# Chunked attention before a routed MoE: window rows of two heads interleaved over the partitions, memory values and sums by one product, and another way from the last gate to the first gather

## The chip, the cores and the metric

The kernel runs on one core of a Trainium2 chip. The metric is device time in microseconds (us) of one execution; smaller is better. TensorE (PE), VectorE (DVE), ScalarE (ACT), GpSimd (POOL) and SyncE (SP) each work through their own instructions in order, and 16 DMA engines serve the queues into which SP, ACT and POOL put transfers. TensorE's granted clock is shown by the profile as a share of full speed.

## The reference

Two stages follow each other. The first is attention over chunks: q, k and v are 4 batches of 8 heads, 768 tokens of 64 values. Each chunk of 32 queries looks at 8 memory rows and a window of 56 tokens around it (16 to the left, its own 32, 8 to the right; cut at the ends), 64 keys in all.

```python
for c in range(nc):                     # 24 chunks of 32
    k_full = np.concatenate([mem_k, k[:, :, l_start:r_end]], axis=2)
    v_full = np.concatenate([mem_v, v[:, :, l_start:r_end]], axis=2)
    scores = scale * np.matmul(q_c, k_full.transpose(0, 1, 3, 2))
    a = np.exp(scores - np.max(scores, axis=-1, keepdims=True))
    a = a / (np.sum(a, axis=-1, keepdims=True) + 1e-09)
    out[:, :, c_start:c_end] = np.matmul(a, v_full)
```

Its output, 3072 tokens of 512 values, goes into a router: `noisy = x @ w_gate + log1p(exp(x @ w_noise)) * noise`; the best two of 8 experts are taken, their weights are a softmax over the two, and each token's result is the weighted sum of `relu(x @ w1[e]) @ w2[e]` (512 to 1024 to 512) over its two experts.

## The kernel before, in words

**Attention** runs in 12 iterations, i = 0 to 11: three per batch, each of 256 tokens (two tiles of 128), all 8 heads. Heads go in pairs; the parity of a head within its pair is `par`.

Loads of v, q and k of a batch are POOL's DMAs (L117, `load_v`, `load_kq`). For v, POOL copies the rows into another order (`spread_v`, L357, two copies), SP writes that to a scratch in DRAM (`vd`, L363), and POOL's DMAs read it back as windows (`window_v`, L372: four per batch, 32 or 24 rows x 24 chunks x 256 values). In the window tile `vb` a head of parity 0 owns partitions 0 to 63 and one of parity 1 owns 64 to 127: 8 memory rows, then 56 window rows; the other half of the columns is zero. The memory rows come by two more POOL DMAs per batch (L367), which copy them from a small tile `mvn` once for every chunk. POOL's own order is written out: every instruction is kept in program order.

TensorE, ScalarE, VectorE and SP follow the order of the program in the loop (`manual_schedule`). For iteration i, TensorE does the scores of i + 1 (`scores`: 8 products with the memory keys, L397, and 32 on 32 columns of the array each, L404), the transposes of the probabilities of i (L425), the transposes of x of i - 1 (L459), the products of `values` for i (8 sums against a two-column tile of ones, L436; 32 products of 32 columns, L442), and the gate of i - 1 (L469, 8 narrow products). In between, `fill` puts the transposes that bring the next batch's q and k into place (L382). VectorE takes the maximum (L412), subtracts it (L414), takes the reciprocal of the sums (L446), multiplies the products by it (L449, twice), copies the gate's logits (L471) and has the routing's small steps. ScalarE does the exponential (L419) and the copies of transposes out of PSUM (L428, L461). Rows of x go to a scratch in DRAM, `xd` (L476), from which the second stage gathers.

The sums have their own tile of PSUM (`small`), which holds the gate's logits as well, at other columns; the products have `ps_o`.

**The way to the gathers.** Tokens are routed in four groups (`Route`: r0, ra, rb with tiles 14 to 19, rc with tiles 20 to 23). Each chooses its two experts (`choose`: 14 small steps of VectorE ending in the one-hot of the pair of experts, `ohp`, L278), takes ranks within a pair by products with triangular and full ones (L284 to L288), turns a rank into a one-hot over 128 places (`slots`, L328, VectorE), spreads six facts per token over the pairs (`values`, L334) and sums them into lists by products (L341). `total` (L318, L322) adds the group's counts to a running count `cum`. The lists are decoded into row numbers to gather (`main_src`, L483) and to write (`main_dst`, L488). r0 and ra are done during the attention, most of rb and all of rc after it. The first gather (L654) waits for `main_src`.

**The MoE** gathers 28 tiles, one per pair of experts, transposes them and does two products for each expert (L697, L709), with results added and written by POOL's indirect DMAs (L660).

The tiles that the change touches are `vb`, `mvn`, `small`, `ps_o`, `rs`, `xd`, `facts`, `vals`, `oh_l` and `listed`.

Of the kernel before, what the change touches and what calls it, by code (L numbers as in the profile page):

```python
# [22 lines left out]
def kernel(  # L23
# [74 lines left out]
    xd = tc.dram_tile([N, Dm // 2], I32, name="xd")  # L98
# [13 lines left out]
    mvs = w_all[0:B * NM, 0, 0:2 * H * D].bitcast(F32).rearrange("p (h d) -> p h d", h=H)  # L112
# [23 lines left out]
    psG = actx.enter_context(tc.psum_pool(name="psG", bufs=1))  # L136
# [15 lines left out]
    for i in range(2):  # L152
        for r0, n in ((0, LC), (LC + S, CH - LC)):
            nc.sync.dma_start(out=vd[i][r0:r0 + n, :], in_=zeros[0:n, :])

# [5 lines left out]
    for b in range(B):  # L161
        nc.sync.dma_start(out=mvs[b * NM:(b + 1) * NM], in_=mem_v[b].rearrange("h m d -> m h d"))
    mvn = keep.tile([B * NM, Dm], BF16, name="mvn")
# [8 lines left out]

    ones2 = const.tile([128, 2], BF16, name="ones2")
    nc.vector.memset(ones2, 0.0)
    nc.vector.memset(ones2[0:64, 0:1], 1.0)
    nc.vector.memset(ones2[64:128, 1:2], 1.0)

# [21 lines left out]
    nc.gpsimd.iota(facts[:, :, 1], pattern=[[1, NG]], base=1, channel_multiplier=0, allow_small_or_imprecise_dtypes=True)  # L199
# [17 lines left out]
    for par in range(2):  # L217
        nc.scalar.copy(vb[1][own(par), 1 - par].rearrange("p (x c) w -> p x (c w)", x=NCH // 2),
                       zeros[own(par), :].unsqueeze(1).to_broadcast([64, NCH // 2, Dm]))
# [9 lines left out]
    class Route:  # L229
# [11 lines left out]
        def noise(self):  # L241
            self.ns = self.tile("ns", E).rearrange("p (n e) -> p n e", e=E)
            nc.scalar.activation(out=self.ns, in_=self.lg[:, :, E:2 * E], func=Act.Exp)
            nc.scalar.activation(out=self.ns, in_=self.ns, func=Act.Ln, bias=1.0)
# [46 lines left out]

        def weights(self, eng):
# [36 lines left out]

        def values(self, eng, lo, hi):  # L330
# [30 lines left out]
    def window_v(b):  # L361
        t, o = vb[b % 2], vd[b % 2]
        nc.sync.dma_start(out=o[LC:LC + S, :].rearrange("(p s) c -> p (s c)", s=SO), in_=vp)  # L363
        for par in range(2):
            p0 = par * 64
            cols = slice(par * 256, (par + 1) * 256)
            pin(nc.gpsimd.dma_start(out=t[p0:p0 + NM, par], in_=mvn[b * NM:(b + 1) * NM, cols].unsqueeze(1).to_broadcast([NM, NCH, 256])))  # L367
        for par in range(2):
            p0 = par * 64
            cols = slice(par * 256, (par + 1) * 256)  # L370
            for r0, n in ((0, CH), (CH, WIN - CH)):
                pin(nc.gpsimd.dma_start(out=t[p0 + NM + r0:p0 + NM + r0 + n, par],  # L372
                                        in_=o[r0:r0 + S, cols].rearrange("(c k) w -> k c w", k=CH)[0:n]))
# [15 lines left out]
    small = psG.tile([128, 4, 128], F32, name="small")  # L389
# [27 lines left out]
    def exps(sc):  # L417
        pb = work.tile([128, 2 * HP, 2, KW], BF16, name="pb")
        nc.scalar.activation(out=pb.rearrange("p x a w -> p (x a) w"), in_=sc, func=Act.Exp, scale=scale)  # L419
        return pb  # L420

    def turn_p(pb):
        p_p = bank([128, 2 * HP, 128], BF16, name="p_p")
        for x in range(2 * HP):
            nc.tensor.transpose(out=p_p[:, x, :], in_=pb[:, x].rearrange("p a w -> p (a w)"),  # L425
                                identity=identb)
# [4 lines left out]
    def values(t, pT, between=None):  # L431
        b, tp = divmod(t, TP)
        ps_g = small[:, t % 2, 0:2 * H].rearrange("p (j h) -> p j h", j=2)
        for x in range(2 * HP):
            j, pair = divmod(x, HP)
            nc.tensor.matmul(out=ps_g[:, j, 2 * pair:2 * pair + 2], lhsT=pT[:, x, :], rhs=ones2,  # L436
                             start=True, stop=True)
        ps_o = psO.tile([128, 2, HP, 2, D], F32, name="ps_o")
        for j in range(2):
            for pair in range(HP):  # L440
                for r in range(4):
                    nc.tensor.matmul(out=ps_o[r * CH:(r + 1) * CH, j, pair], lhsT=pT[:, j * HP + pair, r * CH:(r + 1) * CH],  # L442
                                     rhs=vb[b % 2][:, :, (tp * 2 + j) * 4 + r, pair * D:(pair + 1) * D],
                                     start=True, stop=True, tile_position=(0, r * CH))
        rs = work.tile([128, 2, H], F32, name="rs")
        nc.vector.reciprocal(rs, ps_g)  # L446
        xr = xrow[b % 2][:, 2 * tp:2 * tp + 2]
        for j in range(2):
            nc.vector.tensor_tensor(out=xr[:, j, 0:Dm].rearrange("p (h d) -> p h d", h=H),  # L449
                                    in0=ps_o[:, j].rearrange("p c a d -> p (c a) d"), in1=bc(rs[:, j], D), op=Alu.mult)  # L450
# [4 lines left out]
    def turn_x(xr):  # L455
# [5 lines left out]
        nc.scalar.copy(xT, p_x)  # L461
        return xT

    def gate(t, xT):
        b, tp = divmod(t, TP)
        ps_l = small[:, 2 + t % 2, 0:4 * E].rearrange("p (j e) -> p j e", j=2)
        for j in range(2):
            for kp in range(KP):
                nc.tensor.matmul(out=ps_l[:, j, :], lhsT=xT[:, kp, j, :], rhs=wgn[:, kp, :],  # L469
                                 start=(kp == 0), stop=(kp == KP - 1))  # L470
        nc.vector.tensor_copy(lg_all[:, 2 * t:2 * t + 2, :], ps_l)  # L471

    def keep_x(t, q):
        b, tp = divmod(t, TP)
        g0 = b * SO + 2 * tp
        q.dma_start(out=xd[g0 * 128:(g0 + 2) * 128, :].rearrange("(s p) r -> p s r", p=128),  # L476
                    in_=xrow[b % 2][:, 2 * tp:2 * tp + 2].bitcast(I32))

    def decode(L, n, name):
        t = const.tile([128, n], F32, name=f"{name}_t")  # L480
        nc.vector.scalar_tensor_tensor(out=t, in0=L[:, 1], scalar=128.0, in1=L[:, 0], op0=Alu.mult, op1=Alu.add)
# [486 lines left out]
```

## Time and profile before

| | us |
|---|---|
| median of three executions | 369.55 (367.07 to 370.01) |
| the profiled execution | 367.86 |
| its span | 366.2 |
| first window product (L442) | 32.46 |
| last normalisation (L449) starts | 134.62 |
| first gather is issued (L654) | 147.20 |
| first product of the MoE (L697) | 151.38 |

The profile is one execution. Its page has busy times by engine, 40 slices of the span with a digit per slice for each engine, for the granted clock and for the DMA engines, and groups of instructions by line, with how long one takes and what ended the idle time before it. The trace answers narrower questions: stretches of time, what each engine waited for, a timeline. In the timeline a row gives the start, the time, the engine, the line, what is written from what, the shape, how many instructions the row holds, and in brackets the idle time before it with its releaser. `PEld` is TensorE's loading of weights, which runs beside its products. Line numbers are those of the kernel before.

### The profile page before, as it was taken

What the parts mean: (1) busy time and instruction counts of PE and PEld (TensorE: products, weight loads), DVE (VectorE), ACT (ScalarE), POOL (GpSimd) and SP (SyncE); (2) the same over time, 40 slices, a digit from 0 to 9 for tenths busy, and PEclk for the clock granted to TensorE, in tenths of its full rate; (3) what the DMA queues carried; (4) which work ended last, traced back from release to release, by engine and by line L of the source; (5) the groups of instructions that cost most, each with busy time, mean ns of one, the idle gap of its engine ahead of it and who ended that gap; (6) DMA issues with size and microseconds to landing.
All of it is one profiled execution on the core that took longest, in us unless ns stands there. A gap on an engine that the chain in (4) does not pass through costs nothing.

```text
span 366.2 us, 7045 instructions
## 1 busy us (share of the span) xinstructions
PE 282.3 (77%) x2941; PEld 181.3 (50%) x2941; DVE 171.0 (47%) x344; ACT 136.7 (37%) x189; POOL 134.9 (37%) x181
## 2 busy tenths in 40 slices
PE   0347373766817752599999999999989999999992
PEld 0236363555715641565554455764436675565540
DVE  7656274699766989431223300964300233312231
ACT  8714554463644360034333243222234223234310
POOL 6460473336435014742651453352480032201122
PEclk9995656685775885599999999999999999999997
DMA  8999999999999999379999999991299982100012
GB/s 115 247 155 169 248 162 155 258 199 199 237 176 198 228 225 180 80 147 179 159 186 206 250 184 240 101 215 54 69 154 186 193 185 80 52 2 2 24 43 81
DMA packets 55462, 56.97 MB, mean 156 GB/s; under 512 B 20119, under 2 KB 45783, under 8 KB 55424
## 3 DMA queue, kind: packets, MB, share of 16 engines
q0 software_dynamic: 34240, 46.82, 73.9%
q1 hardware_dynamic: 14048, 6.62, 9.5%
q10 hardware_dynamic: 7136, 3.02, 4.3%
q8 instruction: 25, 0.41, 0.5%
q14 instruction: 13, 0.11, 0.1%
HBM read 70.39 MB, written 13.96 MB: 230 GB/s over the span
## 4 chain that ended last, share of the span: by engine, by line
issue 25%; PE 21%; POOL 8%; DVE 5%; DMA 2%; POOLq 1%; ACT 0%; another core or an unknown queue 0%; DVEq 0%
PE p_h L697 10%; PE p_y L709 9%; POOL out_dram L660 6%; DMA out_dram<-y,main_dst 1%; POOL xt L654 1%; DMA xt<-xd,main_src 1%; PE p_xt L674 1%; DVE h L683 1%; POOL w_all L826 0%; DVE cum L322 0%; DVE w_all L449 0%; POOLq L963 0%; ACT xT L461 0%; DVE oh_l L328 0%
## 5 line engine op out<-in xcount | busy, mean ns | idle before, releaser
L709 PE MATMUL p_y<-w_all,h 128*128 128x512 bf16 x464 | 103.9, 379 | 1.5 <-ACT y L713 1.5
L697 PE MATMUL p_h<-xTt,w_all 128*128 128x256 bf16 (+3 forms) x672 | 102.9, 313 | 1.1 <-issue 0.5
L697 PEld LDWEIGHTS <-w_all 128*128 128x128 bf16 x736 | 69.8, 100 | 37.1 <-issue 1.6
L685 ACT ACTIVATE h<-p_h 128x512 bf16<-128x512 f32 (+1 forms) x81 | 44.5, 551 | 98.6 <-PE p_h L697 90.7
L709 PEld LDWEIGHTS <-h 128*128 128x128 bf16 x464 | 45.3, 98 | 53.2 <-issue 1.8
L683 DVE TENSOR_SCALAR h<-p_h 128x512 bf16<-128x512 f32 (+1 forms) x49 | 31.0, 632 | 85.9 <-PE p_h L697 70.5
L660 POOL DMA_INDIRECT out_dram<-y,main_dst x28 | 30.8, 1101 | 86.0 <-DVE y L715 75.6
L382 PE MATMUL p_t<-identb,w_all 128*64 128x128 bf16 x384 | 19.3, 272 | 30.8 <-DMA w_all<-in_k_dram 14.8
L715 DVE SCALAR_TENSOR_TENSOR y<-p_y,main_w,y 128x512 f32<-128x512 f32 x28 | 21.0, 750 | 37.9 <-PE p_y L709 33.3
L654 POOL DMA_INDIRECT xt<-xd,main_src x28 | 27.5, 982 | 26.3 <-DMA xTt<-xt 13.3
L713 ACT ACTIVATE y<-p_y,main_w 128x512 f32<-128x512 f32 x28 | 19.1, 687 | 38.8 <-PE p_y L709 35.6
L382 PEld LDWEIGHTS <-w_all 128*64 128x64 bf16 x384 | 16.4, 143 | 33.0 <-DMA w_all<-in_k_dram 15.5
L372 POOL DMA_DIRECT2D w_all<-vd x16 | 11.8, 745 | 26.4 <-DMA vd<-vp 25.3
L428 ACT COPY pT<-p_p 128x1024 bf16<-128x1024 bf16 x12 | 12.1, 1010 | 23.5 <-PE p_p L425 23.5
L449 DVE TENSOR_TENSOR w_all<-ps_o,rs 128x512 bf16<-128x512 f32 x24 | 15.5, 686 | 10.5 <-PE ps_o L442 10.0
L536 DVE COPY kT<-p_t 64x768 bf16<-64x768 bf16 x12 | 11.5, 955 | 12.5 <-PE p_t L382 12.4
L419 ACT ACTIVATE pb<-sc 128x1024 bf16<-128x1024 f32 x12 | 12.8, 1062 | 10.9 <-DVE sc L414 10.9
L357 POOL COPY vp<-w_all 128x1536 bf16<-128x1536 bf16 x8 | 11.5, 1467 | 13.3 <-DMA w_all<-in_v_dram 13.3
L442 PE MATMUL ps_o<-w_all,pT 128*32 128x128 bf16 x384 | 10.6, 274 | 6.1 <-issue 5.0
L412 DVE TENSOR_REDUCE mx<-ps_s 128x16 f32<-128x1024 f32 x12 | 14.7, 1223 | 1.2 <-PE ps_s L404 0.9
L414 DVE TENSOR_TENSOR sc<-ps_s,mx 128x1024 f32<-128x1024 f32 x12 | 14.7, 1224 | 0.8
L404 PE MATMUL ps_s<-kT,qT 128*32 128x112 bf16 x384 | 11.2, 274 | 3.6 <-DVE kT L536 2.4
(166 smaller groups left out, 279.3 us busy)
## 6 DMA issues: line engine op xcount, KB each, us to landing
w_all<-in_moe_w_dram POOLq DMA_DIRECT2D x16, 1024.0 KB
w_all<-in_moe_w_dram POOLq DMA_DIRECT2D x8, 512.0 KB
w_all<-in_v_dram POOLq DMA_DIRECT2D x4, 768.0 KB
w_all<-in_k_dram POOLq DMA_DIRECT2D x4, 768.0 KB
w_all<-in_q_dram POOLq DMA_DIRECT2D x4, 768.0 KB
vd<-vp SPq DMA_DIRECT2D x4, 768.0 KB, 6.9
w_all<-vd POOLq DMA_DIRECT2D x8, 384.0 KB
xd<-w_all ACTq DMA_DIRECT2D x11, 256.0 KB, 12.0
```

Of the source, the lines that this page charges most:

```text
L382: nc.tensor.transpose(out=p_t[own(par), s, :], in_=src[:, 2 * pair + par, s * D:(s + 1) * D], identity=identb, tile_position=(0, par * 64))
L412: nc.vector.tensor_reduce(out=mx, in_=s3, axis=AX, op=Alu.max)
L414: nc.vector.tensor_tensor(out=sc, in0=s3, in1=bc(mx, KW), op=Alu.subtract)
L449: nc.vector.tensor_tensor(out=xr[:, j, 0:Dm].rearrange("p (h d) -> p h d", h=H), in0=ps_o[:, j].rearrange("p c a d -> p (c a) d"), in1=bc( ...
L654: i = nc.gpsimd.indirect_dma_start(out=xts[key].bitcast(I32), out_offset=None, in_=xd, in_offset=bass.IndirectOffsetOnAxis(ap=ix, axis=0))
L660: i = nc.gpsimd.indirect_dma_start(out=out, out_offset=bass.IndirectOffsetOnAxis(ap=ix, axis=0), in_=y, in_offset=None, bounds_check=N - 1 ...
L683: nc.vector.tensor_scalar(out=out_, in0=in_, scalar1=0.0, scalar2=None, op0=Alu.max)
L685: nc.scalar.activation(out=out_, in_=in_, func=Act.Relu)
L697: nc.tensor.matmul(out=o, lhsT=w(kp * F + f * 128, 128), rhs=x[:, kp], start=(kp == 0), stop=(kp == KP - 1))
L709: nc.tensor.matmul(out=p, lhsT=h[:, (f * n + j) * 128:(f * n + j + 1) * 128], rhs=w(KP * F + f * Dm, Dm), start=(f == 0), stop=(f == FB - 1))
L713: nc.scalar.activation(out=y, in_=p, func=Act.Copy, scale=weight)
L715: nc.vector.scalar_tensor_tensor(out=y, in0=p, scalar=weight, in1=y, op0=Alu.mult, op1=Alu.add)
```

## The change

*Window.* Row r of a head of parity par now lies on partition 2 x (8 + r) + par, so the rows of two heads alternate over all 128 partitions, and the probabilities are written interleaved to fit. The window DMAs write every second partition.

*Memory values and sums.* The two DMAs per batch that copied memory rows are gone. A new tile `mvz` holds, per batch and pair of heads, the memory values of both parities and one more column each, which is one on that parity's partitions. It is filled at the start by eight small POOL DMAs (L195 after), which stand in POOL's order ahead of `spread_v(0)`, and VectorE writes the columns of ones. One product of the whole array with `mvz` (130 columns) replaces the sums of a pair and adds the memory part; the four window products accumulate on it. The order is now, for each of eight, one whole product and four of 32 columns. Products, sums and the gate's logits share one tile of PSUM (`prods`). The reciprocal is taken in two halves, each ahead of its multiplication.

*Way to the gathers.* `xd` gets a row of zeros ahead of the tokens, so that the row number is one sum of two facts and needs no product and no maximum. The last x is copied in halves, and the exponential of the last gate reads PSUM directly. rc's ranks take rb's counts by products, so `total` for rb goes out of the way. rb's one-hot is done by ScalarE (six squares of a difference, then 1 - x cut at zero); rb's and rc's `values` go from POOL to VectorE, the two facts of the row number first; all of these are summed by 20 products into one tile, to which the part known since iteration 9 is added.

```diff
-    xd = tc.dram_tile([N, Dm // 2], I32, name="xd")
+    xd = tc.dram_tile([128 + N, Dm // 2], I32, name="xd")
...
-    for b in range(B):
-        nc.sync.dma_start(out=mvs[b * NM:(b + 1) * NM], in_=mem_v[b].rearrange("h m d -> m h d"))
-    mvn = keep.tile([B * NM, Dm], BF16, name="mvn")
+    mvz = keep.tile([128, B, HP, 2, D + 1], BF16, name="mvz")
+    nc.vector.memset(mvz, 0.0)
...
+    for par in range(2):
+        for b in range(B):
+            pin(nc.gpsimd.dma_start(out=mvz[par:2 * NM:2, b, :, par, 0:D],
+                                    in_=mem_v[b].rearrange("(c a) m d -> a m c d", a=2)[par]))
...
+        def slots_act(self):
+            n = self.n
+            self.oh_l = self.tile("oh_l", 128, BF16).rearrange("p (n t) -> p n t", t=128)
+            for g in range(n):
+                nc.scalar.activation(out=self.oh_l[:, g], in_=io_l, func=Act.Square, scale=-1.0, bias=self.rr[:, g:g + 1])
+            nc.scalar.activation(out=self.oh_l, in_=self.oh_l, func=Act.Relu, scale=-1.0, bias=1.0)
...
         for par in range(2):
-            p0 = par * 64
-            cols = slice(par * 256, (par + 1) * 256)
-            pin(nc.gpsimd.dma_start(out=t[p0:p0 + NM, par], in_=mvn[b * NM:(b + 1) * NM, cols].unsqueeze(1).to_broadcast([NM, NCH, 256])))
...
             for r0, n in ((0, CH), (CH, WIN - CH)):
-                pin(nc.gpsimd.dma_start(out=t[p0 + NM + r0:p0 + NM + r0 + n, par],
-                                        in_=o[r0:r0 + S, cols].rearrange("(c k) w -> k c w", k=CH)[0:n]))
+                p0 = 2 * (NM + r0) + par
+                pin(nc.gpsimd.dma_start(out=t[p0:p0 + 2 * n - 1:2, par],
+                                        in_=o[r0:r0 + S, par * 256:(par + 1) * 256].rearrange("(c k) w -> k c w", k=CH)[0:n]))
...
-    small = psG.tile([128, 4, 128], F32, name="small")
+    prods = psO.tile([128, 1536], F32, name="prods")
+
+    def prod(j):
+        return prods[:, j * 703:j * 703 + 764].rearrange("p (c w) -> p c w", w=191)[:, :, 0:2 * (D + 1)]
...
-            nc.tensor.matmul(out=ps_g[:, j, 2 * pair:2 * pair + 2], lhsT=pT[:, x, :], rhs=ones2,
-                             start=True, stop=True)
-        ps_o = psO.tile([128, 2, HP, 2, D], F32, name="ps_o")
...
-                                     rhs=vb[b % 2][:, :, (tp * 2 + j) * 4 + r, pair * D:(pair + 1) * D],
-                                     start=True, stop=True, tile_position=(0, r * CH))
-        rs = work.tile([128, 2, H], F32, name="rs")
-        nc.vector.reciprocal(rs, ps_g)
+            nc.tensor.matmul(out=prod(j)[:, pair], lhsT=pT[:, x, :], rhs=mvz[:, b, pair].rearrange("p a d -> p (a d)"),
+                             start=True, stop=False)
+            for r in range(4):
+                nc.tensor.matmul(out=heads(j)[r * CH:(r + 1) * CH, pair, :, 0:D], lhsT=pT[:, x, r * CH:(r + 1) * CH],
+                                 rhs=vb[b % 2][:, :, (tp * 2 + j) * 4 + r, pair * D:(pair + 1) * D],
+                                 start=False, stop=True, tile_position=(0, r * CH))
...
         for j in range(2):
+            nc.vector.reciprocal(rs[:, j], heads(j)[:, :, :, D])
...
-        ps_l = small[:, 2 + t % 2, 0:4 * E].rearrange("p (j e) -> p j e", j=2)
+        ps_l = prods[:, 1408 + t % 2 * 4 * E:1408 + (t % 2 + 1) * 4 * E].rearrange("p (j e) -> p j e", j=2)
...
+        xT = turn_x(xrs.pop(i), True)
         advance(chosen)
         rb.weights(nc.gpsimd)
-        rb.order()
-        rb.values(nc.gpsimd, 0, NV)
-        gate(i, xT)
-        rc.noise()
+        rc.early()
+        gate(i, xT, rc.ns[:, 2:4])
+        rc.late()
         rb.ranks()
-        advance(rb.total())
+        rc.open_ranks(rb)
         chosen = rc.choose()
         advance(chosen, 4)
         advance(rb.place())
+        rb.slots_act()
         advance(chosen)
         rc.weights(nc.gpsimd)
-        rc.values(nc.gpsimd, 0, 2)
-        rc.ranks()
-        rb.slots(nc.vector)
-        rb.lists(0, NV, False)
+        rc.close_ranks()
+        for r in (rb, rc):
+            r.values(nc.vector, 0, 2)
         advance(rc.place())
         rc.slots(nc.vector)
...
+        for r in (rb, rc):
+            for s in range(r.n):
+                for f in range(2):
+                    nc.tensor.matmul(out=p_ids, lhsT=r.oh_l[:, s, :], rhs=r.vals[:, s, f],
+                                     start=(r is rb and s + f == 0), stop=(r is rc and s + f == r.n))
+        nc.vector.tensor_tensor(out=src, in0=p_ids, in1=known, op=Alu.add)
```

121 lines of the change are left out of this document (76 added, 45 removed).

## The prediction

> **What bounds the kernel now.** I read the page's slices first; one digit is 9.2 us.
>
> ```profile
> PE   0347373766817752599999999999989999999992
> ...
> PEclk9995656685775885599999999999999999999997
> DMA  8999999999999999379999999991299982100012
> ```
>
> From the 18th slice on (about 150 us) TensorE is full at a granted clock of 9 tenths; the change touches nothing there. Before it TensorE is busy 3 to 8 tenths at half to full clock, and the DMA engines are full. So the change is decided in the first 150 us. The stretches show the two parts, with these columns after the name: length; busy time of PE, PEld, DVE, ACT, POOL; clock; DMA share; GB/s.
>
> ```profile
> 100.00:134.00 34.00, 18.79 (x463) 15.84 (x463) 24.97 (x57) 17.14 (x23) 7.88 (x12) 0.75 1.14 205
> 134.00:147.00 13.00, 3.94 (x46) 2.78 (x44) 11.57 (x42) 1.47 (x3) 5.60 (x14) 0.58 0.98 187
> ```
>
> In attention VectorE (25.0 of 34 us) is the fullest engine, but not full; in the way to the gathers it is (11.6 of 13). What TensorE waits for stands in the waits (total, times, longest):
>
> ```profile
> PE p_t L382 <- DMA w_all<-in_k_dram: 14.8, 4, 8.5
> PE p_t L382 <- issue: 7.5, 2, 7.2
> ...
> PE ps_o L442 <- issue: 5.0, 1, 5.0
> PE small L469 <- DVE rs L446: 4.6, 3, 2.4
> ```
>
> So at each batch's start it waits for key rows; twice it stands with no releaser (59.2 to 64.2, 103.9 to 111.1); three times the gate product waits for VectorE's normalisation. The timeline shows one iteration that nothing delays, at half clock:
>
> ```profile
> 54.00 0.37 PE L436 MATMUL small<-ones,pT 128*128 128x2 bf16 x8 [0.31 <-ACT pT L428]
> 54.30 0.78 PEld L442 LDWEIGHTS <-pT 128*32 128x32 bf16 x32
> 54.30 1.05 PE L442 MATMUL ps_o<-w_all,pT 128*32 128x128 bf16 x32
> 54.65 0.25 DVE L446 RECIPROCAL rs<-small 128x16 f32<-128x16 f32 x1
> 54.76 1.06 ACT L419 ACTIVATE pb<-sc 128x1024 bf16<-128x1024 f32 x1
> 55.28 0.29 PEld L469 LDWEIGHTS <-xT 128*128 128x128 bf16 x8 [0.20 <-issue]
> 55.28 0.38 PE L469 MATMUL small<-wgn,xT 128*128 128x16 bf16 x8
> 55.42 1.29 DVE L449 TENSOR_TENSOR w_all<-ps_o,rs 128x512 bf16<-128x512 f32 x2 [0.53 <-PE ps_o L442]
> ```
>
> The sums (L436) come first, so the reciprocal runs beside the 32 small products, the gate beside the two multiplications, and the next scores behind it with no wait.
>
> **The change, part by part.** The sum goes against the profiled execution: span 366.2 and 1.66 around it, 367.86 us; the median of the runs, 369.55, lies 0.5% above.
>
> 1. *Products and sums (L436, L442 merged).* Before: 0.37 + 1.05 at half clock, 1.4 us; 0.35 + 0.63 at full, 1.0. After, each of eight groups is one full-array product of 130 columns and four products on 32 columns of the array. In the records the step from full array to 32 columns costs 0.09 to 0.10 us from start to start, the step back 0.15 at full clock and 0.24 at half (between two narrow full products: 0.027). Before has one of each per iteration, after eight. Per group: 0.10 + 0.02 for the four starts + 0.15 or 0.24, near 0.28 or 0.39; eight are 2.25 or 3.1. Plus 1.25 us (1.7 at half clock). Bounds: +0.3 (switches free, 8 x 130 columns as in the 0.62 us of a full-clock L425 row) to +2.2.
>
> 2. *The wait for normalisation.* Sums and values now share one tile, and the gate's logits lie in the same tile. By the compiled waits of the changed kernel the first reciprocal waits for the last of 40 products, and the next gate product for the second multiplication. That is 0.22 + 0.65, twice: 1.75 to 1.85 us (rows L446, L449) in which TensorE stands, and in order behind the gate stand the scores of the iteration after next, whose maximum VectorE then waits for. Before, recip and gate overlapped. TensorE's round is then: transposes 1.2 (0.62 + 0.61 at 120.12) to 1.9 (66.62 to 68.29), wait for pT 0.3 to 0.6, products 2.25 to 3.1, normalisation 1.8, gate 0.35, scores 0.9 to 1.3: 7.1 us at full clock, 9 at half. Reciprocal to reciprocal before: 4.62 (54.65 to 59.27), 4.99 and 4.05 (124.53, 129.52, 133.57). So +2.1 to +4.4 for an iteration that nothing else holds; I take the upper half only where the clock row is at 5 or 6. Lower bound 0: if a transfer or the fetch is late anyway, it hides all.
>
> 3. *Start.* The eight loads of mvz (L195 after) stand on POOL ahead of spread_v(0). By the compiled waits the sixth, seventh and eighth wait for v, k and q of batch 0. Before, the spread began at 9.48 on v alone:
>
> ```profile
> 9.48 2.87 POOL L357 COPY vp<-w_all 128x1536 bf16<-128x1536 bf16 x2 [2.71 <-DMA w_all<-in_v_dram]
> ...
> 19.56 2.95 POOL L372 DMA_DIRECT2D w_all<-vd x4 [4.63 <-DMA vd<-vp]
> ```
>
> q is there by 20.19, where TensorE's wait of 2.9 us for it ends, sooner without the vd write beside it: about 17.5, then an issue (0.68) and the spread at 18.4, +8.9. Write and windows then have the queues more to themselves: 2.9 + 5.2 (768 KB at the 150 GB/s of the page's mean) + 11 (19.56 to 32.46 less the memory rows) puts values(0) near 37, before 32.46: +4.5. The POOL queue behind it (loads of batch 1, its spread, windows) moves with it. VectorE's memset of mvz, the odd column and its copy lie beside DMA waits: nothing, or at most the 2 us by which kT's copies (15.39) wait for the mvz loads. Bounds 0 to +8.9.
>
> 4. *Transfers saved.* The two copies of memory rows per batch go: 192 KB in 4096-byte packets of 0.44 us median, 1.2 to 3 us of the queues for each of batches 1 to 3, and 1.3 us of POOL issue. It counts where a transfer is last: k at 45.75, windows before 64.17, q at 70.88, k at 75.65 and 102.74.
>
> 5. *Walk.* With these durations and waits, laid out by hand engine by engine, the ends of the scores come, before and after: iteration 3: 51.9, 57.5; 4: 56.8, 66.2; 5: 66.7, 75.0; 6: 80.9, 90.7; 7: 88.5, 98.4; 8: 95.4, 106.6; 9: 114.75, 120.5. [...] So +5.75 by iteration 9. From there nothing waits for a DMA: iterations 9 to 11 and the last products take 19.0 us before (114.75 to 133.77) and 26.6 after, four rounds with +1.9 each on average: +7.6. At that point +13.4.
>
> 6. *Way to the gathers.*
>
> ```profile
> 137.43 1.87 POOL L334 TENSOR_TENSOR vals<-ohp,facts 128x1008 bf16<-128x1008 bf16 x1
> ...
> 137.86 1.49 DVE L322 TENSOR_TENSOR cum<-cum,red 128x28 bf16<-128x28 bf16 x1
> ```
>
> cum took 1.49 where 0.19 is its size elsewhere (120.90), while POOL's vals ran: it goes, with the 0.44 of the sum before it, in part hidden behind the exponential: -1.4. xT in halves: -0.5. The second reciprocal: +0.4. From rc's choice (ohp 142.61) to the ids: before 3.36 (142.91 to 146.27); after vals 0.45 + 0.33 on VectorE, ohr 0.26, rank 0.27, oh_l 0.85, twenty narrow products 0.5, one add 0.2: 2.9, -0.45. From ids to the gather's issue 0.93 before, -0.3 at best. ScalarE's seven one-hot instructions (2.2 us by its rows of 0.23 and 1.02) lie beside rc's choice, 3.3 us of VectorE; with that cover gone they would cost up to 2. Together -2.3, between -0.5 and -3.3.
>
> Sum: 367.86 + 5.75 + 7.6 - 2.3 = 378.9, so 379.
>
> [...]
>
> **The rivals.** *A, the transfers set the pace.* The windows of a batch take 8.9 to 10.7 us of full queues, and DMA stands at 9 in nearly every slice to 150 us. If the windows, spread over twice as many partitions, land in the time of the queue's better slices (248 to 258 against 155 to 170 GB/s), and the memory copies are gone, each batch's keys come 2 to 5 us sooner, the 7.2 us stand does not return, and TensorE, which has slack in every batch before the last, loses its lengthening there. It decides if k of batch 3 is there by 99 instead of 102.7: iteration 9's scores then end at 106, 8.7 sooner, and with +7.6 and -2.3 that is 364.5; with 1.5 a round instead of 1.9, 363. For it: 6.6 us of waits for q, 14.8 for k. Against it: the start puts all these loads behind by 4.5, and each load of the loop is issued behind buffers that the slower rounds free. [...]
>
> *B, the wait overlaps.* VectorE had 9 us of slack in 34; if the records' step costs shrink in a mixed order, only about +0.8 a round is left: +3 at iteration 9, +3 behind it, -2.3: 371.5. Against it: the wait of the gate for normalisation is in the compiled program, and already costs 2.4 at 87 us where it occurs.
>
> *C, the stands return, or the clock stays at half.* TensorE standing 1.8 us each round could keep the clock row at 5: +1.9 a round for four rounds more, or the 7.2 us stand comes back behind k of batch 3 (+5): 384 to 387. For it: the row shows 5s and 6s wherever it idles. [...] The stretch of 100 to 134 shows 0.75, with half clock also around 125 to 128, where the longest gap is 2.0 us, so the measurement decides.
>
> **How the numbers follow.** A measurement can tell about 1% from no change. Chances: forecast 0.46 (373 to 383), A 0.21 (358 to 366; 0.17 of it faster by over 1%), B 0.14 (0.08 within 1%), C 0.19. So faster 0.17, same 0.12, slower 0.71. The range 364 to 387 leaves out the better half of A and the worst of C. The likeliest alone: 373 to 383.
>
> **What would show it.** Right: spread_v(0) starts near 18; the gate row names the multiplication as its releaser, about 1.8 us before it in most iterations; the merged products take over 2 us; the round is 7 us or more; cum is gone ahead of the gathers. Wrong: a first gather before 147, windows that land in under 8 us, products of 1.4 us, or keys that arrive before TensorE asks.

## The result and the profile after

The changed kernel takes 408.5 us (median of four runs, 407.16 to 409.52) against 369.78 us before on the same chip: a ratio of 1.1085, with a 95% interval of 1.1033 to 1.1136. The forecast was 379.0 us with a range of 364 to 387: the sign came true, the size did not. The profiled execution of after took 409.52 us with a span of 407.9.

The same three rows of the page, now with one digit for 10.2 us:

```profile
PE   0247407767758697745799999999998999999992
...
PEclk9999997566568555555899999999999999999998
DMA  8859999592199990002799999999118998110012
```

TensorE's full stretch (PE 9 at a clock of 9) begins at the 21st slice, near 204 us, where before it began at the 18th, near 156. Ahead of it the clock row holds a 5 or a 6 in eleven of the thirteen slices from the 7th to the 19th, and the DMA row, full to 150 us before, has holes: 2 and 1 around 100 us, 0 from 153 to 184. So in the second half of attention the queues' bandwidth doesn't limit this kernel. The stretches (columns as before: length, busy PE, PEld, DVE, ACT, POOL, clock, DMA share, GB/s) say it in numbers:

```profile
60.00:100.00 40.00, 29.19 (x500) 22.78 (x501) 21.24 (x44) 21.82 (x27) 11.38 (x17) 0.68 0.88 184
100.00:134.00 34.00, 25.19 (x420) 18.87 (x421) 20.09 (x41) 15.08 (x19) 9.03 (x10) 0.65 0.77 157
134.00:180.00 46.00, 33.48 (x442) 22.71 (x439) 28.14 (x69) 16.14 (x22) 6.02 (x14) 0.50 0.49 99
```

In the last one TensorE is busy 73% of the time and was granted half clock for all of it. What engines waited for (total, times, longest) shows three rows that matter:

```profile
ACT xT L489 <- DMA w_all<-vd: 22.4, 2, 16.8
...
PE prods L497 <- ACT xT L489: 21.4, 3, 14.1
...
PE prods L497 <- DVE w_all L474: 12.3, 8, 1.9
```

The third is the wait that the prediction put in term 2. The first is new, and the second was 2.9 us before: ScalarE's copy of the transposed x (L489) stands for a window DMA, and TensorE's gate (L497) stands for that copy. A copy from PSUM needs no window, so what holds it must lie ahead of it in ScalarE's queue. The timeline (start, length, engine, work, idle time before and its releaser):

```profile
58.71 2.88 POOL L385 COPY vp<-w_all 128x1536 bf16<-128x1536 bf16 x2 [5.09 <-DMA w_all<-vd]
58.74 0.38 ACTq L506 DMA_DIRECT2D xd<-w_all  x1
59.16 1.01 ACT L489 COPY xT<-p_x 128x1024 bf16<-128x1024 bf16 x1 [16.82 <-DMA w_all<-vd]
60.07 1.36 ACT L448 ACTIVATE pb<-sc 128x1024 bf16<-128x1024 f32 x1
60.22 0.29 PEld L497 LDWEIGHTS <-xT 128*128 128x128 bf16 x8 [14.33 <-ACT xT L489]
60.22 0.38 PE L497 MATMUL prods<-wgn,xT 128*128 128x16 bf16 x8 [14.15 <-ACT xT L489]
```

Directly ahead of the copy, on ScalarE's own DMA queue, is the issue of the store of x to DRAM (`keep_x`, L506). It is held until the next batch's window DMAs have landed, then issues in 0.38 us, and the copy, the exponential and TensorE's gate all follow within 1.5 us. Before, a store of the same loop issued 0.08 us after ScalarE's copy of pT began:

```profile
57.80 1.01 ACT L428 COPY pT<-p_p 128x1024 bf16<-128x1024 bf16 x1 [1.98 <-PE p_p L425]
57.88 0.37 ACTq L476 DMA_DIRECT2D xd<-w_all  x1
```

In the compiled program of after, three stores (x of iterations 0, 2 and 5) each wait for all four window DMAs of the batch that is being loaded (1, 2 and 3); the trace has them issue at 58.74, 85.15 and 119.89. Each later spread on POOL waits for the windows ahead of it, 10.2 us in two waits. Before, no store and no spread waits for a window. The store reads other columns of `w_all` than the windows write. That it takes every second partition of a tile for an overlap with a tile of other columns is my inference from where the waits appear; the traces show the waits, not their reason.

The rest went as the prediction has it, or slower. The start:

```profile
17.90 0.54 POOL L195 DMA_DIRECT2D mvz<-in_mem_v_dram  x1 [3.37 <-DMA w_all<-in_q_dram]
18.44 2.88 POOL L385 COPY vp<-w_all 128x1536 bf16<-128x1536 bf16 x2
20.00 1.42 DVE L554 CAST mvz<-odd 128x32 bf16<-128x32 f32 x1 [5.14 <-DMA mvz<-in_mem_v_dram]
```

VectorE stands 5.14 us for the loads of `mvz`, so that its copies of kT (L560) start at 21.43, before at 15.39. TensorE's transposes wait for these copies, 6.3 us at one place:

```profile
PE p_t L405 <- DVE kT L560: 6.7, 2, 6.3
```

A round late in attention, at half clock; one group is a whole product (L464) and four narrow ones (L467), and the last line ahead of the gap loads the next group's:

```profile
144.69 0.29 PE L464 MATMUL prods<-mvz,pT 128*128 128x130 bf16 x1
144.91 0.11 PEld L467 LDWEIGHTS <-pT 128*32 128x32 bf16 x4
144.91 0.30 PE L467 MATMUL prods<-w_all,pT 128*32 128x128 bf16 x4
145.14 0.10 PEld L464 LDWEIGHTS <-pT 128*128 128x128 bf16 x1
...
155.25 0.21 DVE L473 RECIPROCAL rs<-prods 128x8 f32<-128x8 f32 x1 [1.76 <-PE prods L467]
155.49 0.69 DVE L474 TENSOR_TENSOR w_all<-prods,rs 128x512 bf16<-128x512 f32 x1
156.10 0.20 DVE L473 RECIPROCAL rs<-prods 128x8 f32<-128x8 f32 x1
156.33 0.69 DVE L474 TENSOR_TENSOR w_all<-prods,rs 128x512 bf16<-128x512 f32 x1
157.07 0.36 PE L497 MATMUL prods<-wgn,xT 128*128 128x16 bf16 x8 [1.88 <-DVE w_all L474]
```

A group takes 0.45 us from start to start (144.69 to 145.14), eight 3.6. Then TensorE stands 1.88 us while VectorE normalises. And the way to the gathers:

```profile
184.53 0.19 DVE L677 TENSOR_TENSOR main_src<-p_ids,known 128x28 int32<-128x28 f32 x1 [0.49 <-PE p_ids L675]
...
185.55 1.69 POOL L706 DMA_INDIRECT xt<-xd,main_src  x1 [2.67 <-DVE facts L322]
```

Where the time went, by the start of the scores' maximum on VectorE, the last normalisation and the end of the span (us). The column "blocks" is the first experiment below:

| | before | forecast | after | blocks |
|---|---|---|---|---|
| maximum, iteration 2 | 35.07 | | 41.20 | |
| iteration 3 | 52.18 | | 69.36 | 55.34 |
| iteration 5 | 69.45 | | 90.42 | 73.86 |
| iteration 8 | 95.69 | | 123.98 | 107.29 |
| iteration 9 | 115.05 | +5.75 | 140.66 (+25.6) | 124.51 (+9.5) |
| last normalisation | 134.62 | +7.6 more | 175.13 (+14.9 more) | 158.14 (+14.1 more) |
| to the end of the span | 231.6 later | -2.3 | 232.8 (+1.2) | 230.2 (-1.4) |

For after, 25.6 + 14.9 + 1.2 = 41.7 us, the difference of the two profiled executions (409.52 less 367.86).

### The profile page after: what moved, and what is told of

It reads as the page before. It is cut to its first block, busy times and chain, and to the rows that moved or that the text cites. A ratio compares the mean times of both kernels' runs of the same rounds, so it can differ in the third digit from the quotient of the medians.

```text
span 407.9 us, 7080 instructions
## 1 busy us (share of the span) xinstructions
PE 316.8 (78%) x2942; PEld 198.4 (49%) x2963; DVE 173.2 (42%) x354; ACT 142.6 (35%) x198; POOL 132.1 (32%) x179
## 4 chain that ended last, share of the span: by engine, by line
PE 32%; issue 26%; DMA 15%; POOL 11%; DVE 8%; ACT 5%; POOLq 1%; ACTq 0%; DVEq 0%
PE p_h L749 10%; PE p_y L761 8%; DMA w_all<-vd 6%; POOL out_dram L712 6%; DMA w_all<-in_q_dram 3%; PE prods L467 3%; PE prods L464 3%; DMA w_all<-in_v_dram 2%; POOL w_all L395 2%; DVE w_all L474 2%; PE p_p L454 2%; DVE kT L575 2%; ACT pT L457 2%; PE ps_s L433 1%; PE p_t L405 1%
## 5 line engine op out<-in xcount | busy, mean ns | idle before, releaser
L761 PE MATMUL p_y<-w_all,h 128*128 128x512 bf16 x446 | 102.5, 379 | 2.3 <-ACT y L765 1.3
L405 PE MATMUL p_t<-identb,w_all 128*64 128x128 bf16 x384 | 21.2, 291 | 18.0 <-DMA w_all<-in_k_dram 8.4
L497 PE MATMUL prods<-wgn,xT 128*128 128x16 bf16 x96 | 4.6, 175 | 34.6 <-ACT xT L489 21.4
L464 PE MATMUL prods<-mvz,pT 128*128 128x130 bf16 x96 | 26.1, 272 | 3.6 <-ACT pT L457 3.6
L405 PEld LDWEIGHTS <-w_all 128*64 128x64 bf16 x384 | 18.6, 157 | 19.9 <-issue 10.5
L467 PE MATMUL prods<-w_all,pT 128*32 128x128 bf16 x384 | 26.9, 270 | 0.0
L497 PEld LDWEIGHTS <-xT 128*128 128x128 bf16 x96 | 4.2, 105 | 36.0 <-ACT xT L489 21.9
L489 ACT COPY xT<-p_x 128x1024 bf16<-128x1024 bf16 x11 | 11.2, 1017 | 27.8 <-DMA w_all<-vd 22.4
L448 ACT ACTIVATE pb<-sc 128x1024 bf16<-128x1024 f32 x12 | 16.3, 1357 | 6.8 <-DVE sc L443 6.8
L473 DVE RECIPROCAL rs<-prods 128x8 f32<-128x8 f32 x24 | 4.9, 202 | 30.4 <-PE prods L467 30.4
L385 POOL COPY vp<-w_all 128x1536 bf16<-128x1536 bf16 x8 | 11.5, 1468 | 17.9 <-DMA w_all<-vd 10.2
```

The source lines that it names most:

```text
L405: nc.tensor.transpose(out=p_t[own(par), s, :], in_=src[:, 2 * pair + par, s * D:(s + 1) * D], identity=identb, tile_position=(0, par * 64))
L464: nc.tensor.matmul(out=prod(j)[:, pair], lhsT=pT[:, x, :], rhs=mvz[:, b, pair].rearrange("p a d -> p (a d)"), start=True, stop=False)
L467: nc.tensor.matmul(out=heads(j)[r * CH:(r + 1) * CH, pair, :, 0:D], lhsT=pT[:, x, r * CH:(r + 1) * CH], rhs=vb[b % 2][:, :, (tp * 2 + j) * ...
L761: nc.tensor.matmul(out=p, lhsT=h[:, (f * n + j) * 128:(f * n + j + 1) * 128], rhs=w(KP * F + f * Dm, Dm), start=(f == 0), stop=(f == FB - 1))
```

## The experiments

The theory: the overrun is the store's wait on ScalarE's queue, added to rounds that are longer than forecast because the clock stays at half. The rival: the rounds alone (gate's wait and switches of the array) make the difference, and the store only stands where TensorE would have stood anyway. The runs shared their chips with runs of the kernel before; ratios are to those.

**Blocks of 64 partitions, all else as after.**

```diff
-                p0 = 2 * (NM + r0) + par
-                pin(nc.gpsimd.dma_start(out=t[p0:p0 + 2 * n - 1:2, par],
+                p0 = par * 64 + NM + r0
+                pin(nc.gpsimd.dma_start(out=t[p0:p0 + n, par],
...
-        pb = work.tile([128, 2 * HP, KW, 2], BF16, name="pb")
+        pb = work.tile([128, 2 * HP, 2, KW], BF16, name="pb")
```

> The changed kernel with the window's rows in blocks of 64 partitions again (and mvz, the probabilities and the column of ones to fit); the merged products, the loads of mvz and the new way to the gathers stay. Theory: writing every second partition made the program wait where nothing is shared: each store of x and each spread of v waited for the four window transfers, and these for the stores, and the store's wait stood on ScalarE ahead of xT. The trace charges 21.4 us of TensorE's gate waits to it. So 380 to 390 us, the store no longer waits for windows, and xT follows p_x within 2 us. Rival 1, the interleaved layout costs by moving data (exponential 1.36 us in place of 1.06, slower transfers): 400 to 405. Rival 2, the merged products and the gate's wait are the bulk and what ScalarE waited for only hid them: 398 or more.

394.85 us, ratio 1.0718 [1.0647, 1.0789]: 13.7 less than after. No wait of xT for a window is left, and the gate's wait is there in eleven of twelve rounds:

```profile
PE prods L497 <- DVE w_all L474: 18.0, 11, 1.9
```

Both effects exist. Above the 380 to 390 expected, so the rounds too cost more than thought.

**Before, with the interleaved window alone** (windows, memory rows, probabilities and the columns of ones for it; products, gate and way to the gathers as before).

```diff
-                pin(nc.gpsimd.dma_start(out=t[p0 + NM + r0:p0 + NM + r0 + n, par],
+                p0 = 2 * (NM + r0) + par
+                pin(nc.gpsimd.dma_start(out=t[p0:p0 + 2 * n - 1:2, par],
...
-        pb = work.tile([128, 2 * HP, 2, KW], BF16, name="pb")
+        pb = work.tile([128, 2 * HP, KW, 2], BF16, name="pb")
```

> The kernel before with the interleaved window alone: rows of the two parities on alternate partitions, memory rows copied there as before, the probabilities interleaved, ones to fit. Sums, products and the way to the gathers as before. Theory: 385 to 395 us, with stores of x that wait for windows. Rival 1, only the data moves differently: 370 to 375, with an exponential of 1.36 us. Rival 2, the layout costs nothing: within 1% of 369.8.

399.48 us, 1.0858 [1.0784, 1.0932], +30.7 us:

```profile
PE small L465 <- ACT xT L457: 52.4, 4, 22.6
ACT xT L457 <- DMA w_all<-vd: 51.4, 3, 22.8
```

The layout alone brings the wait, three times, once for each later batch. 52.4 us of standing at TensorE's gate cost 30.7, since other waits of TensorE got shorter: that for key rows is 8.2 us where before it was 14.8, and the two stands without a releaser (7.2 and 5.0) are gone.

**After, with the stores on SP's queue.**

```diff
-                keep_x(i - 1, nc.scalar)
+                keep_x(i - 1, nc.sync)
```

> The changed kernel with the stores of x of the loop issued by SyncE in place of ScalarE; the wait stays in the program but nothing that computes stands behind it. Theory: most of the 21.4 us of TensorE's wait for xT goes, less what then waits for the spread of v: 385 to 395. If the windows themselves were late (rival 1): 404 to 409.

394.02 us, 1.0681 [1.0603, 1.0760], 14.5 less than after and not to be told from the blocks. One queue was changed, no transfer, no layout, no wait of the store for the windows: so what the layout costs in after is that ScalarE stands behind the store.

**Before, with the new way to the gathers alone** (the part of the diff from `xd` on).

> The kernel before with the new way to the gathers alone (row of zeros, one sum per token, one-hot by ScalarE, ranks opened early, values on VectorE). Theory: from the last normalisation's start to the first gather's issue it takes 10.4 us as in the changed kernel, 12.6 before: -2.2, 367 to 368. Rival: the way was only shorter because the queues were empty 40 us later: 369 to 371.

368.32 us against 368.76, 1.0005 [0.997, 1.004]. From the last normalisation (135.25) to the first gather 10.40 us, before 12.58: -2.18, as forecast. In the total it can't be seen:

```profile
145.53 0.86 DVE L367 TENSOR_TENSOR vals<-ohp,facts 128x672 bf16<-128x672 bf16 x1
145.65 1.70 POOL L711 DMA_INDIRECT xt<-xd,main_src  x1 [2.68 <-DVE facts L327]
...
156.63 1.63 PE L754 MATMUL p_h<-xTt,w_all 128*128 128x256 bf16 x10 [2.23 <-issue]
```

The first gather's issue takes 1.70 us beside VectorE's `vals` where before it took 1.14, so that by the last normalisation the first MoE product is 1.7 us earlier instead of 2.2 (150.29 less 135.25 against 151.38 less 134.62). Then TensorE stands 2.23 us at 154.4 with no releaser in the trace. After has the same stand, 2.4 us, and ends 1.2 us later by the normalisation. Every other kernel here with the new way has one of 1.9 to 2.6 us, but for the profiled run of the blocks: it has 1.20 us there, behind a copy of VectorE, and ends 1.4 us earlier. What the stand is isn't settled.

**Blocks, with the gate's logits in a bank of their own.**

```diff
-        ps_l = prods[:, 1408 + t % 2 * 4 * E:1408 + (t % 2 + 1) * 4 * E].rearrange("p (j e) -> p j e", j=2)
+        ps_l = bank([128, 2, 2 * E], F32, name="ps_l")
```

> The kernel of e1 (blocks of 64 partitions, the rest as changed) with the gate's logits in a PSUM tile of their own, from the ring that the transposes use. Theory: of e1's 26 us over the kernel before, 18.0 are TensorE standing ahead of the gate until the second normalisation is done (11 times 1.6 to 1.9); with it gone a round is 7.5 us of TensorE at half clock in place of 9.3, and the clock may rise: 372 to 380. Rival: the products' own length is the bulk and VectorE follows them anyway (the scores wait for the same products): 388 or more.

374.78 us, 1.0173 [1.0116, 1.0229], 20.1 less than the blocks. The gate's wait for the normalisation is gone. Its row summed to 18.0 us, so about all of it is gained. The clock comes back as well; what that adds is not shown apart, since the executions of the blocks spread over 5 us. The stretch from 100 to 126 us, blocks and then this kernel:

```profile
100.00:126.00 26.00, 18.89 (x304) 14.73 (x300) 15.88 (x37) 11.26 (x16) 5.17 (x10) 0.57 1.16 208
```

```profile
100.00:126.00 26.00, 19.01 (x329) 13.20 (x323) 18.32 (x40) 12.70 (x17) 5.59 (x9) 0.74 1.16 213
```

**Blocks, with the eight whole products first and the 32 narrow ones behind them.** Each narrow product starts anew, so the memory values don't reach the output.

```diff
-                             start=True, stop=False)
+                             start=True, stop=True)
+        for x in range(2 * HP):
+            j, pair = divmod(x, HP)
...
-                                 start=False, stop=True, tile_position=(0, r * CH))
+                                 start=True, stop=True, tile_position=(0, r * CH))
```

> The kernel of e1 with the eight whole-array products first and the 32 narrow ones behind them, each group started anew; the same 40 products in the same shapes, one switch of shape in place of eight. It leaves out the memory values in the result (they are overwritten), not the work for them. Theory: the products take 3.6 us in e1 at half clock, 0.45 for each group; in order of shape 1.03 + 1.05 and one switch, about 2.3: 1.3 us a round, twelve rounds, most of it on the path: 378 to 386. Rival: the time is that of the products and not of the switches: 392 or more.

372.94 us, 1.0118 [1.0067, 1.0168]: 21.9 less than the blocks, more than expected, though the gate still waits:

```profile
PE prods L499 <- DVE w_all L476: 20.4, 11, 3.3
```

Eight groups take 3.6 us in the rows above; here the eight whole products take 0.99 us from start to start at half clock (114.57 to 115.56) and the 32 narrow ones 1.06 behind them. That is 1.55 us less in each of twelve rounds, 19 in all. The clock from 100 to 126 us is 0.76, against 0.57 in the blocks.

**Both together** (the memory values left out as well).

> Both edits of e5 and e6 on the kernel of e1 (the memory values left out as in e6). Theory: nothing of the attention's loop is then left but the later start (+3.4 us at the first scores) and the way to the gathers (-1): 367 to 374. Rival: another wait of the merged tile remains (the next products must wait for the normalisation's reading): 378 or more.

363.15 us, 0.9860 [0.9818, 0.9902], below what was expected. So the two costs of the merged products, 20.1 and 21.9 apart, are 31.7 together: they overlap. With neither of them the time lies below that of before.

**Blocks, with the loads of mvz behind the first spread** (and no longer ahead of it).

```diff
         spread_v(0)
+        for par in range(2):
+            for b in range(B):
+                pin(nc.gpsimd.dma_start(out=mvz[par * 64:par * 64 + NM, b, :, par, 0:D],
+                                        in_=mem_v[b].rearrange("(c a) m d -> a m c d", a=2)[par]))
         window_v(0)
```

> The kernel of e1 with the eight loads of mvz issued behind the spread of v of batch 0 and ahead of its windows. Theory: the spread starts at 9.5 us again, VectorE's copies of k wait for nothing, the first scores' maximum starts at 25 in place of 28.5; 3 us sooner at the first gather if the loop carries it, 391 to 392. Rival: later waits for transfers swallow it: 394 to 396.

388.56 us, 1.0558 [1.0502, 1.0613], 6.3 less than the blocks; the spread starts at 9.24 instead of 17.53, and VectorE's copies of kT at 15.16 instead of 20.52. More than the 3 expected: the start doesn't sink into later waits.

**The whole function without these costs.** Blocks, logits apart, loads later, and per iteration three products of zeros that start each bank of `prods`; then the eight whole and, behind them, the 32 narrow products accumulate on the zeros, and the array switches once.

```diff
+        for c in range(3):
+            nc.tensor.matmul(out=prods[:, c * 512:min(c * 512 + 512, 1408)], lhsT=zeros[:, 0:128], rhs=zeros[:, 0:min(512, 1408 - c * 512)],
+                             start=True, stop=False)
...
-                             start=True, stop=False)
+                             start=False, stop=False)
+        for x in range(2 * HP):
+            j, pair = divmod(x, HP)
...
-                                 start=False, stop=True, tile_position=(0, r * CH))
+                                 start=False, stop=x in (2, 5, 7), tile_position=(0, r * CH))
```

> All parts mended, nothing left out: blocks of 64 partitions as in e1, the gate's logits apart as in e5, the loads of mvz later as in e8, and the order of shapes of e6 made right by a start of each of the three PSUM banks with zeros (three products of 512, 512 and 384 columns, while TensorE waits for pT), on which eight whole products and then 32 narrow ones add up. Theory: e7's 363.2 less the 4 to 6 us that the start was worth in e8, plus up to 0.6 us a round where the zeros do not hide in the wait for pT (0.3 to 0.6): 358 to 363, faster than the kernel before by 1.5 to 3%. Rival: the zeros wait for the second normalisation of the round before and bring the wait back: 370 or more.

359.77 us (359.39 to 360.66), 0.9773 [0.9737, 0.9809]. Its round:

```profile
109.95 0.54 PE L458 MATMUL prods<-zeros 128*128 128x512 bf16 x2
...
110.33 0.63 PE L462 MATMUL prods<-mvz,pT 128*128 128x130 bf16 x8
...
110.89 0.64 PE L467 MATMUL prods<-w_all,pT 128*32 128x128 bf16 x32
```

1.2 us of products at full clock, where after has 3.6 at half and 2.7 at full; the zeros start ahead of pT's arrival (110.2), and no row of the waits has the gate behind the normalisation. The clock row:

```profile
PEclk9999859889859855799999999999999999999998
```

**The new way to the gathers on before, with the gate apart.**

```diff
-        ps_l = small[:, 2 + t % 2, 0:4 * E].rearrange("p (j e) -> p j e", j=2)
+        ps_l = bank([128, 2, 2 * E], F32, name="ps_l")
```

> The kernel of e4 (attention as before, new way to the gathers) with the gate's logits in a tile of their own. Theory: the kernel before already loses 4.6 us in three waits of the gate for the reciprocal; half of it is on the path: 365 to 367. Rival: other waits take its place, 368 to 369.

369.77 us, 1.0015 [0.9974, 1.0057]: nothing gained. In before's order the reciprocal runs beside the 32 narrow products and the gate beside the multiplication, so its gate row is short (4.6 us), and two stands without a releaser (6.4 and 6.1 us) are here as there (5.0 and 7.2).

**Interleaved window on before, stores on SP** (the second experiment, with the third's edit).

> The kernel of e2 (the kernel before with the interleaved window alone, 399.5 us) with the stores of x in the loop issued by SyncE. Theory: what the layout costs is the store's wait for the windows, on ScalarE ahead of xT; off ScalarE, 372 to 380 are left (the spread of v still waits for windows, the exponential is 0.3 longer). Rival: the layout's data movement and the later spread are half of it: 383 or more.

364.97 us, 0.9878 [0.9814, 0.9942]: 34.5 less than the same kernel with the stores on ScalarE, and less than expected. So the layout's cost on the kernel before is the queue, all of it.

**The ninth kernel with the interleaved layout again** (windows, probabilities, `mvz` and `odd` as in after).

> The kernel of e9 (359.8 us) with the window, mvz, the probabilities and the columns of ones interleaved over the partitions again. Theory: rounds are short there, so the store's wait is bare as in e2: 385 to 395. Rival: with the products mended the layout costs only what it did between e1 and the changed kernel, 13.7 us: 370 to 376.

384.35 us, 1.0418 [1.0351, 1.0484], 24.6 more than with blocks:

```profile
ACT xT L489 <- DMA w_all<-vd: 36.6, 3, 19.0
...
PE ps_l L497 <- ACT xT L489: 35.8, 3, 18.7
```

With the rounds short the layout costs 24.6, and the runs below show that this is the store's wait; in after, whose rounds were long, the wait is worth 14.5. Each hides part of the other: layout alone +30.7, the rest alone +26.1 (blocks), together +38.7.

**What the layout itself does.** Three kernels with the stores on SP: before, the ninth, and the twelfth.

> The kernel before with the stores of x in the loop issued by SyncE, nothing else. If the layout made e11 fast: 368 to 370, and e11's 365.0 is 4 us of the layout. If the place of the stores did (ScalarE's queue loses 11 issues of 0.37 us ahead of xT): 364 to 366, and the layout is worth nothing.

> The kernel of e9 (359.8 us) with the stores on SyncE. If the place of the stores helps: 356 to 358.5. If not: 359 to 361.

> The kernel of e12 (zeros first, interleaved layout, 384.4 us) with the stores on SyncE. Theory: the 24.6 us by which e12 is slower than e9 are the store's wait on ScalarE: 358 to 364. If the layout itself helps, as the transfers over more partitions would: 2 us or more below e14. Rival: the spread of v, which still waits for the windows, holds it at 368 or more.

Before with the stores on SP takes 367.30 us, 0.9931 [0.9898, 0.9965]; the ninth 359.80, 0.9736 [0.9697, 0.9776]; the twelfth 357.43, 0.9684 [0.9641, 0.9727]. The layout without the queue's wait is thus worth 2.3 us on before (364.97 against 367.30, on different chips) and 2.4 on the ninth. The intervals overlap, so that it gains is not settled; that it costs nothing by itself is. The last has the lowest median, 3.2% under the kernel before, with the layout, the merged products and the new way to the gathers all in it.

## Why the prediction was wrong in size

Two steps failed. The sum had no term for a wait that the layout brought, and the rounds of steps 1 and 2 were taken too short. Without the wait the time would still lie above the range of 364 to 387: the blocks take 394.85.

**A wait that was not in the sum.** The forecast kernel is, but for one thing, the blocks: their maxima at iterations 3, 4 and 8 (55.34, 63.86, 107.29) lie within 2.4 us of the ends of scores in the walk of step 5 (57.5, 66.2, 106.6), which in before are 0.3 us ahead of the maximum at 3 and 8. After leaves the walk at iteration 3, by 12 us, which is where the first store of x stands behind the windows. The change did say where rows lie, and I priced that as bandwidth only. The waits that the prediction names are those of computing engines and of POOL's loads; the DMA issues that stand in ScalarE's queue are not among them. The wait is 14.5 of the overrun of 29.5 us (408.5 less 379.0); rival C, which held the slower cases, had nothing of it.

**Step 2, the round.** The wait of 1.8 us is as forecast (1.88), and the mechanism was right. The round I took, 7.1 to 9 us with the upper half only where the clock row says so, was 8.9 to 10.3 (maxima at 140.66, 151.01, 159.90); the clock is 0.50 throughout, and at half clock the sum had 9. So the four last rounds cost 14.9 us instead of 7.6. That is the first half of rival C, which I gave +1.9 a round; it measured +1.8. Between 141 and 170 us TensorE never stands longer than 1.9 us at a time, and the clock doesn't leave 0.50. The clock had fallen at 132 us: it is 1.00 from 126 to 132 and 0.51 from 132 to 135. The longest stand of TensorE in the ten microseconds ahead of the fall is this one:

```profile
130.91 0.34 PE L497 MATMUL prods<-wgn,xT 128*128 128x16 bf16 x8 [1.88 <-DVE w_all L474]
```

So the fall came with no stand over 1.88 us, and in the rounds from 141 to 170 us, which stop for up to 1.9 us, no rise came. How much idle time counts is not shown. Nor did the row of before have 5s and 6s wherever TensorE idles, as rival C read it: of its seven slices with a PE of 4 or less, three are at 5 or 6, one at 7 and three at 9.

**Step 1, the switches.** Per group 0.45 us at half clock and 0.335 at full, forecast 0.39 and 0.28 (the terms given add up to 0.36 and 0.27); eight are 3.6 and 2.7 us for 3.1 and 2.25. The step back was right (0.22 and 0.16). The step to the narrow products was not: 0.10 in before, where it stands behind products of 2 and 16 columns (L436, L397), and here, behind one of 130 columns, 0.22 at half clock and 0.16 at full. Measured apart, few switches (-21.9 us) are worth as much as the gate's wait (-20.1); the prediction had them at 1.25 to 1.7 and 1.8 a round, about equal, so the proportion was right and both were too small. That the clock makes the difference is my reading; no run shows it apart.

**Step 3, the start.** Spread at 18.44, forecast 18.4: right. The first product of values came at 35.45, forecast near 37, so +3.0 us where the sum had +4.5, and that it came out near is partly luck. The sum lets this product wait for the windows, which in after had landed by 35.12; the product waits for pT. It is late because VectorE's copies of kT started 6.0 us later than before, behind the loads of `mvz`, where the prediction allowed at most 2. The start was worth 6.3 us in total by the eighth experiment, which takes both delays away.

**Step 4 and rival A, the transfers.** From the first to the last landing of a batch's four windows the traces have, for batches 0 to 3, 6.2, 5.9, 6.1 and 6.3 us in after and 6.9, 9.1, 7.8 and 7.4 in blocks with the same products; 6.0, 5.6, 7.0 and 5.5 in the twelfth kernel and 6.4, 8.8, 8.0 and 9.0 in the ninth, its form in blocks. Rival A wanted about a third less (the time at 248 to 258 GB/s against that at 155 to 170). The traces agree in part: summed over the batches it is 22% and 25% less, for batch 0 alone 11% and 5%, and what else the queues carried differs between the kernels, so no run shows apart what the partitions do to a transfer's rate. The windows did land in under 8 us, a sign of being wrong that the prediction had named. Rival A's gain did not follow: the layout is worth at most 2.4 us in total.

**Step 5, catching up.** The +5.75 takes the stands of 5.0 and 7.2 us as gone, and in after they are: the one wait of TensorE without a releaser in its trace is the 2.4 us in the MoE. What the two were, and why they went, no run shows. But from iteration 8 to 9 the blocks take 17.2 us and the walk had 13.9: behind the gate, which waits 1.88, stand 72 transposes of k and q (4.3 us at half clock) and the copies of kT that the scores wait for.

**Step 6, the way to the gathers.** -2.16 us up to the gather, forecast -2.3: right, and right in its mechanism. Carrying it whole to the total was wrong: alone it is worth nothing that can be measured (1.0005, with an interval of 0.997 to 1.004).

**Rival B** has nothing for it: the gate's wait is there in nearly every round.

In sum, on the profiled execution of the blocks (389.88): 3.7 us more at iteration 9, 6.5 in the rounds, 0.9 behind them make the 11 above 379 (the median of the blocks, 394.85, is another 5 above this execution, the lowest of five); the store's wait comes on top. Not priced at all was the exponential, which takes 1.36 us with interleaved output instead of 1.06. It can't be seen in the totals (the eleventh and the last kernel have it and have the lower medians of their pairs).

## What to carry to other kernels

When a layout changes, read in the compiled program the waits of everything that touches the same buffer, the DMA issues in the queues of computing engines above all: one store that waits there holds all that its engine does next, and moving it to an idle queue is a change of one word (here 34.5 us on the kernel before with the layout, 14.5 on the changed one). Where products of two array widths accumulate, start each bank once with zeros and order the rest by width (the order alone was worth 21.9 us of the blocks); and give what must not wait a bank of its own (20.1 us of them). Rounds of 9 to 10 us with a stop of 1.9 us in each ran at half clock here, so price such a round at half clock until the trace shows the other.

## What was unexpected of the hardware

- Half clock held for 46 us at 73% busy TensorE (0.50, 134 to 180 us of after). From 100 to 126 us the blocks had 0.57, and 0.74 and 0.76 when either the stop or the switches were taken away.
- The clock fell from 1.00 to 0.51 at 132 us of after with no stand of TensorE over 1.88 us in the ten microseconds ahead.
- From the start of a whole product of 130 columns to that of four narrow ones 0.22 us pass at half clock, and 0.23 to the next whole one (144.69, 144.91, 145.14); eight whole products in a row take 0.12 us each (0.99 us in the sixth run).
- ScalarE's exponential of 128x1024 takes 1.36 us when it writes every second element of bf16, 1.06 when it writes them in order.
- The first indirect DMA's issue on POOL takes 1.70 us where VectorE's product of bf16 (`vals`) starts with it, 1.14 where that product ends 0.18 us behind its start.
